# A fused hash attention and SwiGLU kernel on one core: five small moves in its slot plan

## The chip, the cores and the metric

The kernel runs on one core of one Trainium2 chip. The metric is the device time of one execution in microseconds, the median of several runs. A core has a matrix engine (TensorE, "PE" in the profile, with its weight loads as "PEld"), a vector engine (DVE), a scalar engine (ACT), a general engine (POOL) and a queue engine (SP), from which most DMA transfers are issued. Every engine works through its own list of instructions in order, and waits where an instruction needs something that another engine or a transfer has not finished. The matrix engine writes only to PSUM, and DVE or ACT read it from there.

## The reference, cut to what matters

The inputs q, k and v have shape (4, 8, 768, 64): four batches, eight heads, 768 tokens, 64 dimensions per head. A random projection of 6 columns gives each query and key 6 sign bits, and a query attends only to keys with the same bits:

```python
q_bits = (np.einsum('bhsd,dk->bhsk', q, proj) > 0)
mask = q_bucket[:, :, :, None] == k_bucket[:, :, None, :]
scores = np.where(mask, scale * np.matmul(q, k.transpose(0, 1, 3, 2)), -1e9)
attn = softmax(scores)          # with 1e-9 added to the sum
x = np.matmul(attn, v)          # heads side by side: (3072, 512)
xn = x / sqrt(mean(x * x) + 1e-6) * rms_g
out = (silu(xn @ w_gate) * (xn @ w_val)) @ w_out
```

The gate and value weights are 512 x 1536, the output weight is 1536 x 512.

## The kernel before, in words

The work is cut into 8 units. A unit is one half (384 queries) of one batch; units 0 and 1 belong to batch 0, units 2 and 3 to batch 1, and so on. A unit has 8 heads, and each head's 768 keys are handled in three chunks of 256, so a unit has 24 chunks. The program is one long list of **slots**, one chunk each, 192 in all (`NS = 24` to a unit). Slot t issues, on each engine's list, the score products of chunk t+1 (`scores`, line 321: two matmuls into `s_ps`), the exponential of chunk t on ACT (`probs`, line 333), and then whatever the table `plan[t]` holds. The helper `at(0, t, f, ...)` puts a step into that table; steps of one slot run in the order in which they were put there. Nothing reorders this list afterwards; buffers are handed out by the framework, and an instruction waits until its buffer is free.

What the plan holds, by name:

- **Loads.** `load_natural`, `load_v` and `load_blocks` (lines 94, 103, 117) are issued from SP, in order, together with the sends of bits and the stores of results. All q, k and v tiles share 8 buffers (`lpool`). `load_w` (line 520) brings weights in from POOL's queue.
- **Turning.** q and k are needed with the head dimension on the partitions. Batch 0 and the first two pairs of heads of batch 1 are turned on PE (`turn_pe`, line 148, copied out of PSUM by DVE at line 150), the other ten pairs on DVE (`turn_dve`, lines 174 and 181). `cast_part` and `cast_pool` (lines 164, 194) then write them as 16-bit numbers into the tile `QK`, mostly on POOL.
- **Hashes.** The projection runs on PE: `hash_direct` (line 222, tile `d_ps`) for the pairs turned on PE, `hash_one` (line 202) for the ten others. DVE cuts the sign bits out (`signs`, line 211, tile `bits`), and SP sends them by DMA into rows 64 to 69 of `QK` (lines 261 and 281). With the bits appended to the head dimension the score product carries the mask, so the first scores of a pair of heads wait for its bits. `hash_direct` needs the last copy of the turned q, and two of the three PSUM banks of the pool `gps`, which it shares with turned tiles, gates, values and projections.
- **Values.** `v_prep` (line 290) writes v as 16-bit numbers, `v_sum` (lines 296 to 298, POOL) and `v_mean` (line 306, tile `m_ps`, copied to `cvb` at line 309) give a sum over all keys that goes into every output.
- **Attention output.** `av` (line 346, tile `o_ps`) multiplies probabilities and values, in two parts in the slots 3n+4 and 3n+5 for the n-th head of the list. After a pair of heads, `attn_out` (lines 360 to 372) adds `cvb` (`otmp`), takes reciprocals (`rcp`), and writes x and its squares (`sq`), the last two on POOL, but for the last pair of unit 0 on DVE. There is one `o_ps` buffer, so the next pair's `av` waits for `otmp`. `sumsq` (line 376) sums the squares.
- **Norm.** `norm_scale` (lines 388, 392) gives 1/rms, on DVE and then POOL; `norm` (line 401) scales the three thirds of x (128 tokens each) on DVE; `turn_x` (line 408) turns each third on PE, and the result is copied to `xnT` with the gain, by DVE (line 414) or, for one third of units 0 and 7, in four pieces by ACT (line 412).
- **Feed-forward.** `gate` and `value` (line 425, tiles `g_ps`, `v_ps`), with a tanh on ACT (line 433) and two DVE products (lines 442, 443), then `project` (line 454, `y_ps`) and `store` (ACT copy at line 466, DMA at 467).

Unit 0's norm comes earliest: its eight heads run in front (two of them before two heads of unit 1), its x is turned in slot `TX = 37`, and from slot 38 on the feed-forward work of earlier units fills PE beside the attention of later ones. `spread` divides that work over the slots of a unit by weights (330 for scores, 216 per projection matmul, 1000 for a hash and so on); a step in `inserts` (the hashes of ten pairs and the six `v_mean` steps) is put in at the first boundary at or behind its slot. For those ten pairs the table `spots` gives the slot of the load, of the turns of k and of q, and of the hash. `behind_norm` moves a pair's casts, and its `v_prep` and `v_sum`, from the first slots of a unit, where the previous unit's norm is computed, to the unit's slot 7.

The lines that the change touches, and what calls them:

Of the kernel before, what the change touches and what calls it, by code (L numbers as in the profile page):

```python
# [16 lines left out]
H = 8  # L17
# [16 lines left out]
def kernel(  # L34
# [12 lines left out]
    nc = tc.nc  # L47
# [265 lines left out]
    x, xn, xnT = {}, {}, {}  # L313
# [69 lines left out]
    rstds = {}  # L383

    def norm_scale(u):

        ss = spool.tile([128, 3], FP32, name="ss")
        nc.vector.tensor_reduce(
            out=ss, in_=ssp[u % 2].rearrange("p h c -> p c h"), op=ALU.add, axis=AX.X
        )  # L390
        rstd = spool.tile([128, 3], FP32, name="rstd")
        nc.gpsimd.tensor_tensor(out=rstd, in0=ss, in1=mhalf, op=ALU.pow)
        rstds[u] = rstd

    def norm(u):
        if u not in rstds:
            norm_scale(u)
        rstd = rstds.pop(u)
        xn[u] = npool.tile([128, 3, DMODEL], FP16, name="xn")
        for c in range(3):  # L400
            nc.vector.tensor_scalar_mul(xn[u][:, c, :], x[u][:, c, :], rstd[:, c : c + 1])

    def turn_x(u, c, act=False):
        if c == 0:
# [122 lines left out]
    NS = 24  # L527
# [5 lines left out]
    def at(w, s, f, *a):  # L533
        plan[NS * w + s].append(lambda: f(*a))
# [43 lines left out]
    at(0, 0, second_head)  # L578
    at(0, 1, cast_part, 0, 0, "q", 1)
    at(0, 1, v_prep, 0, 0)  # L580
    for hp, s0 in ((1, 2), (2, 8), (3, 14)):
        at(0, s0, new_pair, 0, hp)
        at(0, s0, turn_pe, 0, hp, 0, "k")
        at(0, s0 + 1, turn_pe, 0, hp, 1, "k")
        at(0, s0 + 1, cast_pool, 0, hp, "k")
        at(0, s0 + 2, turn_pe, 0, hp, 0, "q")
        at(0, s0 + 3, turn_pe, 0, hp, 1, "q")
        at(0, s0 + 3, cast_part, 0, hp, "q", 0, 0, 2, nc.vector)
        at(0, s0 + 3, cast_part, 0, hp, "q", 1)
        at(0, s0 + 4, hash_pair, 0, hp)  # L590
        if hp == 1:
            at(0, s0 + 5, send_pair, 0, hp, (1,))
            at(0, s0 + 5, move_head, 0, hp, 0)
        else:
            at(0, s0 + 5, send_pair, 0, hp)
# [1 line left out]
    at(0, 1, load_natural, nc.sync, 0, 3, "q")  # L597
    at(0, 2, load_v, nc.sync, 0, 2)
    at(0, 2, load_v, nc.sync, 0, 3)
    at(0, 8, v_prep, 0, 1, nc.vector)  # L600
    at(0, 13, v_prep, 0, 2, nc.vector)
    at(0, 19, v_prep, 0, 3, nc.vector)
    for hp, t in enumerate((4, 16, 21, 31)):
# [5 lines left out]
        at(0, 39 + 3 * i, load_w, wo, moe_w_out, 6 * i, 6)  # L609


    for hp, ts in ((0, (8, 22, 23, 24, 25, 24, 26, 26, 28, 42)), (1, (17, 27, 28, 29, 30, 29, 41, 32, 33, 43))):
        tl, ts = ts[0], ts[1:]
        for w in "kq":
            at(0, tl, load_natural, nc.sync, 1, hp, w)
        at(0, tl, load_v, nc.sync, 1, hp)
        at(0, ts[0], new_pair, 1, hp)
        for t, hh, w in zip(ts[0:4], (0, 1, 0, 1), "kkqq"):
            at(0, t, turn_pe, 1, hp, hh, w)
        at(0, ts[4], cast_pool, 1, hp, "k")  # L620
        at(0, ts[5], cast_pool, 1, hp, "q")
        if hp == 0:
            at(0, ts[6], hash_pair, 1, hp)
            at(0, ts[7], send_pair, 1, hp)
        at(0, ts[8], v_prep, 1, hp)
        at(0, ts[8], v_sum, 1, hp)

    spots = {
# [11 lines left out]
    TX = 37  # L640
# [7 lines left out]

    at(0, 24, nc.gpsimd.tensor_scalar_mul, gcol, gcol, float(DMODEL) ** 0.5)
    for n, (u, h) in enumerate(order):  # L650
        for part in range(2):
            at(0, 3 * n + 4 + part, av, u, h, part)
        if h % 2:
            if (u, h) == (0, H - 1):

                at(0, 3 * n + 5, o_step, u, h // 2, nc.vector)
                at(0, 3 * n + 5, s_step, u, h // 2)
                at(0, 3 * n + 5, norm_scale, u)
                at(0, 3 * n + 6, hash_only, 1, 1)
                at(0, 3 * n + 6, hash_signs, 1, 1)  # L660
                at(0, 3 * n + 6, norm, u)
                at(0, TX + 1, send_pair, 1, 1)
                at(0, TX - 1, idle, 2, bank)
                at(0, TX, idle, 1, bank)
                for c in range(3):
                    at(0, TX, turn_x, u, c, c == 1)
                continue
            at(0, 3 * n + 5, o_step, u, h // 2)
            at(0, 3 * n + (10 if h < 7 else 7), s_step, u, h // 2)

# [3 lines left out]
    SCORES, AV, PROJ, FEED, TURN, HASH, MEAN = 330, 290, 216, 324, 220, 1000, 120  # L674
    inserts = {spot[3]: (HASH, hash_one, *pair) for pair, spot in spots.items()}
    for b in (1, 2, 3):
        inserts[2 * b * NS + 3] = (MEAN, v_mean, b, 0, 4)
        inserts[2 * b * NS + 18] = (MEAN, v_mean, b, 2, 4)

    def spread(t0, n, pieces):  # L680
        fixed = [SCORES + (AV if (t - 1) % 3 < 2 else 0) for t in range(t0, t0 + n)]
# [23 lines left out]
    for u in range(7):  # L705
        gates = [
            (FEED, f is gate and part == 0, [(0, f, u, ft, part)])
            for ft in range(NF) for f in (gate, value) for part in range(2)
        ]
        if u == 0:  # L710
            t0 = TX + 1
            spread(t0, 2 * NS - t0, gates)
            continue
        t0 = NS * (u + 1)
        at(0, t0 + 4, norm, u)
        pieces = []
        for i in range(9):
            c, n = divmod(i, 3)
            steps = [(0, project, u - 1, c, 4 * n, 4 * n + 4)]
            if n == 2:  # L720
                steps.append((1, store, u - 1, c))
            pieces.append((4 * PROJ, True, steps))
            if i in (6, 7):
                pieces += [
                    (TURN, False, [(0, turn_x, u, c)]) for c in ((0,), (1, 2))[i - 6]
                ]
        spread(t0, NS, pieces + gates)
# [2 lines left out]

    def behind_norm(t):

        return t - t % NS + 7 if 2 <= t % NS < 7 else t

    for (b, hp), (load, kturns, qturns, _) in spots.items():
        at(0, load, load_blocks, nc.sync, b, hp)
        at(0, load, load_v, nc.sync, b, hp)
        at(0, kturns[0], new_pair, b, hp)
        for w, turns in (("k", kturns), ("q", qturns)):
            for i, t in enumerate(turns):  # L740
                at(0, t, turn_dve, b, hp, w, i, len(turns))
            at(0, behind_norm(turns[-1] + 1), cast_pool, b, hp, w)
        t = behind_norm(qturns[-1] + 2)
        at(0, t, v_prep, b, hp)
        at(0, t, v_sum, b, hp)
# [17 lines left out]
    for c in range(2):  # L763
        project(6, c, 0, NF)
        store(6, c)
    norm(7)
    project(6, 2, 0, 4)
    for c, f0, f1 in ((0, 4, 7), (1, 7, 9), (2, 9, NF)):
# [41 lines left out]
```

## Time and profile before

| | |
|---|---|
| median of 3 runs | 339.15 us (339.05 to 339.28) |
| the profiled execution | 339.4 us, of which 337.6 us are the span from first to last instruction |
| busy over the span | PE 98%, DVE 70%, ACT 66%, POOL 44% |
| granted TensorE clock | full in all 40 slices of the span |
| moved by DMA | 30.92 MB, 92 GB/s on the mean |

The profile is one execution, recorded by the hardware. Its page gives busy times by engine, the chain of work that ended last (followed backwards from the last instruction to whatever released it), and groups of instructions by source line. Further views of the same trace are used: the timeline, in which equal neighbours of one engine are merged and a bracket gives the idle time just before and what ended it; the chain in order of time; busy time by stretch; and one tile's or one line's instructions. Times within the trace count from the start of the span. The ends of matmuls are modelled, so matmuls that follow each other overlap in these rows; the chain's rows give the time from one to the next. An instruction that waits for several things is put down to the one that came last.

### The profile page before, as it was taken

How to read it: one execution, taken by the hardware profiler on the slowest of the kernel's cores; microseconds unless marked ns; L12 is line 12 of the kernel's file. 1: busy time of each engine (PE TensorE's matmuls, PEld its weight loads, DVE VectorE, ACT ScalarE, POOL GpSimd, SP SyncE). 2: the span in 40 equal slices, each digit the busy share in tenths (PEclk: the TensorE clock that was granted, in tenths of full speed). 3: DMA queues.
4: the chain of work that ended last, by engine and by line, in shares of the span. 5: the costliest groups of instructions: out<-in, count | busy, mean ns of one | idle time of the engine just before them, and what ended most of it. 6: DMA issues, size and time to landing. Idle time of an engine off the chain costs nothing.

```text
span 337.6 us, 7795 instructions
## 1 busy us (share of the span) xinstructions
PE 329.3 (98%) x3004; PEld 198.3 (59%) x3004; DVE 235.8 (70%) x492; ACT 224.0 (66%) x325; POOL 149.2 (44%) x201
## 2 busy tenths in 40 slices
PE   8898999999999999999999999999999999999996
PEld 4566756655566555655656556565656666664554
DVE  2898696777869558875788658884776446674870
ACT  2788886666677767777667667776667767754322
POOL 3457949427553632746373523738371121112000
PEclk9999999999999999999999999999999999999999
DMA  7944899982818527070816118000200010001002
GB/s 234 328 142 150 129 152 210 229 143 50 185 23 159 109 87 150 12 136 26 148 71 106 42 65 171 7 1 19 83 3 3 2 62 34 0 2 68 28 0 93
DMA packets 79692, 30.92 MB, mean 92 GB/s; under 512 B 64988, under 2 KB 76712, under 8 KB 79656
## 3 DMA queue, kind: packets, MB, share of 16 engines
q1 hardware_dynamic: 75528, 25.45, 31.6%
q0 software_dynamic: 3680, 4.72, 8.4%
q8 instruction: 23, 0.38, 0.5%
q10 hardware_dynamic: 448, 0.27, 0.2%
q14 instruction: 13, 0.11, 0.1%
HBM read 28.32 MB, written 6.29 MB: 103 GB/s over the span
## 4 chain that ended last, share of the span: by engine, by line
PE 91%; DVE 4%; DMA 2%; ACT 1%; issue 1%; SPq 0%; DVEq 0%
PE v_ps L425 18%; PE g_ps L425 18%; PE s_ps L321 17%; PE y_ps L454 17%; PE o_ps L346 10%; PE d_ps L202 3%; PE t_ps L148 2%; PE x_ps L408 2%; PE d_ps L222 2%; DMA qL<-in_q_dram 1%; PE z_ps L515 1%; DVE bits L211 1%; PE y_ps L473 1%; DMA QK<-bits 1%; ACT psb L333 1%
## 5 line engine op out<-in xcount | busy, mean ns | idle before, releaser
L333 ACT ACTIVATE psb<-s_ps,ebias 128x768 f16<-128x768 f32 x192 | 167.5, 899 | 25.0 <-PE s_ps L321 24.3
L321 PE MATMUL s_ps<-QK 70*128 70x384 f16 x384 | 93.9, 326 | 2.5 <-DMA QK<-bits 1.1
L433 ACT ACTIVATE t<-g_ps 128x384 f32<-128x384 f32 x96 | 47.1, 490 | 56.3 <-PE g_ps L425 56.1
L425 PE MATMUL g_ps<-xnT,wg 128*128 128x384 f16 x384 | 82.5, 325 | 0.2
L425 PE MATMUL v_ps<-xnT,wv 128*128 128x384 f16 x384 | 81.7, 325 | 0.3 <-DVE a L442 0.2
L442 DVE SCALAR_TENSOR_TENSOR a<-t,g_ps 128x384 f32<-128x384 f32 x96 | 52.8, 550 | 28.2 <-ACT t L433 26.8
L454 PE MATMUL y_ps<-wo,ht 128*128 128x512 f16 x276 | 68.0, 378 | 0.0
L367 POOL TENSOR_TENSOR x<-otmp,rcp 128x384 f32<-128x384 f32 x31 | 25.7, 829 | 93.1 <-DVE rcp L365 92.9
L346 PEld LDWEIGHTS <-psb 128*128 128x128 f16 x1152 | 52.1, 97 | 16.3 <-issue 1.3
L443 DVE SCALAR_TENSOR_TENSOR ht<-a,v_ps 128x384 f16<-128x384 f32 x96 | 53.2, 554 | 11.7 <-PE v_ps L425 3.2
L346 PE MATMUL o_ps<-vl,psb 128*128 128x65 f16 x1152 | 56.3, 193 | 0.5 <-DVE otmp L360 0.5
L321 PEld LDWEIGHTS <-QK 70*128 70x128 f16 x384 | 34.5, 98 | 36.4 <-issue 11.0
L425 PEld LDWEIGHTS <-wv 128*128 128x128 f16 x384 | 35.2, 97 | 22.6 <-issue 1.8
L425 PEld LDWEIGHTS <-wg 128*128 128x128 f16 x384 | 34.6, 97 | 21.2 <-DVE xnT L414 0.6
L454 PEld LDWEIGHTS <-ht 128*128 128x128 f16 x276 | 24.7, 97 | 22.7
L372 POOL TENSOR_TENSOR sq<-x 128x384 f32<-128x384 f32 x31 | 25.6, 826 | 2.4
L194 POOL CAST QK<-kT 64x768 f16<-64x768 f32 x20 | 16.4, 820 | 22.6 <-DVE kT L174 7.7
L466 ACT COPY ysb<-y_ps 128x512 f32<-128x512 f32 x23 | 13.5, 585 | 18.6 <-PE y_ps L454 18.6
L360 DVE TENSOR_TENSOR otmp<-o_ps,cvb 128x390 f32<-128x390 f32 x32 | 17.9, 559 | 10.0 <-PE o_ps L346 9.7
L194 POOL CAST QK<-qT 64x768 f16<-64x768 f32 x20 | 16.5, 825 | 18.5 <-DVE qT L181 17.1
L376 DVE TENSOR_REDUCE ssp<-sq 128x3 f32<-128x384 f32 x32 | 16.9, 529 | 9.9 <-POOL sq L372 9.9
L414 DVE TENSOR_TENSOR xnT<-x_ps,gcol 128x512 f16<-128x512 f16 x22 | 14.5, 685 | 5.8 <-PE x_ps L408 5.8
(71 smaller groups left out, 262.8 us busy)
## 6 DMA issues: line engine op xcount, KB each, us to landing
vn<-in_v_dram SPq DMA_DIRECT2D x16, 384.0 KB
out_dram<-ysb SPq DMA_DIRECT2D x23, 256.0 KB
qL<-in_q_dram SPq DMA_DIRECT2D x40, 96.0 KB
kL<-in_k_dram SPq DMA_DIRECT2D x40, 96.0 KB
kn<-in_k_dram SPq DMA_DIRECT2D x5, 384.0 KB
qn<-in_q_dram SPq DMA_DIRECT2D x5, 384.0 KB
wg<-in_moe_w_gate_dram POOLq DMA_DIRECT2D x2, 768.0 KB, 7.8
wv<-in_moe_w_val_dram POOLq DMA_DIRECT2D x2, 768.0 KB, 9.6
```

What stands on the lines that cost most here:

```text
L194: nc.gpsimd.tensor_copy(QK[b, 2 * hp + hh, "h"][0:64, o : o + S], src[64 * hh : 64 * hh + 64, :])
L321: nc.tensor.matmul(ps[:, j, 0:HALF], QK[b, h, "h"][0:KROWS, S + jt * 128 : S + (jt + 1) * 128], QK[b, h, "h"][0:KROWS, half * HALF : (half ...
L333: nc.scalar.activation(psb[u, h][:, 2 * ch : 2 * ch + 2, :], sps.pop((u, i))[:, :, 0:HALF], AF.Exp, bias=ebias, scale=ESCALE,)
L346: nc.tensor.matmul(o[:, c, hh, 0:65], psb[u, h][:, jt, c * 128 : (c + 1) * 128], vls[b % 2][:, h, 2 * (jt % 3) + jt // 3 if b in PARITY el ...
L360: nc.vector.tensor_add(tmp[:, :, :, 0:65], o[:, :, :, 0:65], cvb[b % 2][:, 2 * hp : 2 * hp + 2, 0:65].unsqueeze(1).to_broadcast([128, 3, 2 ...
L367: eng.tensor_mul(xd.rearrange("p c (h d) -> p c h d", h=2), tmp[:, :, :, 0:64], r.to_broadcast([128, 3, 2, 64]),)
L372: eng.tensor_mul(sq, xd, xd)
L425: nc.tensor.matmul(ps, w[:, kt, fs], xnT[u][:, kt, :], start=(kt == 0), stop=(kt == 3))
L433: nc.scalar.activation(t, fbank[u, ft, "g_ps"], AF.Tanh, scale=0.5)
L442: nc.vector.scalar_tensor_tensor(out=a, in0=t, scalar=1.0, in1=g, op0=ALU.add, op1=ALU.mult)
L443: nc.vector.scalar_tensor_tensor(out=ht[u][:, ft, :], in0=a, scalar=0.5, in1=vv, op0=ALU.mult, op1=ALU.mult)
L454: nc.tensor.matmul(y, ht[u][:, ft, c * 128 : (c + 1) * 128], wo[:, ft, :], start=(ft == 0), stop=(ft == NF - 1),)
```

## The change

Five moves; no arithmetic is added or taken away.

1. **Unit 0's last sums a slot sooner.** The two `av` parts of unit 0's last head go from slots 31 and 32 to 30 and 31, and with them `o_step`, `s_step`, `norm_scale` (32 to 31), the hash of batch 1's second pair and `norm` (33 to 32). `norm` scales only two thirds of unit 0's x on DVE; the third one is scaled by ACT in slot 37 (`norm_third` with `nc.scalar.mul`), ahead of the turns. Of the three copies to `xnT`, ACT now makes the third instead of the second.
2. **Batch 0's last pair (heads 6 and 7)** is turned, hashed and sent one slot sooner (14 to 13 and on, hash 18 to 17, send 19 to 18), and the `v_prep` of batch 0's second pair, which is on DVE, goes from slot 8 to slot 10.
3. **A load behind bits.** The loads of batch 1's second pair go from slot 17 to slot 20.
4. **Two hashes of batch 1 a slot later.** Pair 2 from 50 to 51, pair 3 from 60 to 61; pair 3's turns go from slots 57, 57, 58, 59 to 55, 56, 57, 58. Since slot 51 held a `v_mean`, the first `v_mean` of batches 1, 2 and 3 goes from a unit's slot 3 to its slot 5.
5. **Casts behind norms.** `behind_norm` now also moves what stands in a unit's slot 1. That is the cast of k of (batch 1, pair 2), from slot 49 to 55, and `v_prep` with `v_sum` of (2, 0), (2, 2) and (3, 2), from slots 73, 97 and 145 to 79, 103 and 151.

```diff
     def norm(u):
         if u not in rstds:
             norm_scale(u)
-        rstd = rstds.pop(u)
         xn[u] = npool.tile([128, 3, DMODEL], FP16, name="xn")
-        for c in range(3):
-            nc.vector.tensor_scalar_mul(xn[u][:, c, :], x[u][:, c, :], rstd[:, c : c + 1])
+        for c in range(3 if u else 2):
+            norm_third(u, c, nc.vector.tensor_scalar_mul)
+
+    def norm_third(u, c, mul):
+        mul(xn[u][:, c, :], x[u][:, c, :], rstds[u][:, c : c + 1])
...
-    for hp, s0 in ((1, 2), (2, 8), (3, 14)):
+    for hp, s0 in ((1, 2), (2, 8), (3, 13)):
...
-    at(0, 8, v_prep, 0, 1, nc.vector)
+    at(0, 10, v_prep, 0, 1, nc.vector)
...
-(1, (17, 27, 28, 29, 30, 29, 41, 32, 33, 43))
+(1, (20, 27, 28, 29, 30, 29, 41, 32, 33, 43))
...
-        (1, 2): (34, (48, 48), (49, 49), 50),
-        (1, 3): (45, (57, 57), (58, 59), 60),
+        (1, 2): (34, (48, 48), (49, 49), 51),
+        (1, 3): (45, (55, 56), (57, 58), 61),
...
+        t = 3 * n + 4 - ((u, h) == (0, H - 1))
         for part in range(2):
-            at(0, 3 * n + 4 + part, av, u, h, part)
+            at(0, t + part, av, u, h, part)
...
-                at(0, 3 * n + 6, hash_only, 1, 1)
-                at(0, 3 * n + 6, hash_signs, 1, 1)
-                at(0, 3 * n + 6, norm, u)
+                at(0, t + 2, hash_only, 1, 1)
+                at(0, t + 2, hash_signs, 1, 1)
+                at(0, t + 2, norm, u)
+                at(0, TX, norm_third, u, 2, nc.scalar.mul)
...
-                    at(0, TX, turn_x, u, c, c == 1)
+                    at(0, TX, turn_x, u, c, c == 2)
...
-        inserts[2 * b * NS + 3] = (MEAN, v_mean, b, 0, 4)
-        inserts[2 * b * NS + 18] = (MEAN, v_mean, b, 2, 4)
+        for s, hp in ((5, 0), (18, 2)):
+            assert 2 * b * NS + s not in inserts
+            inserts[2 * b * NS + s] = (MEAN, v_mean, b, hp, 4)
...
     def behind_norm(t):
-        return t - t % NS + 7 if 2 <= t % NS < 7 else t
+        return t - t % NS + 7 if 1 <= t % NS < 7 else t
```

More of the change, by code (lines that the diff above doesn't have):

```diff
@@ L609 @@
         at(0, 39 + 3 * i, load_w, wo, moe_w_out, 6 * i, 6)
-    for hp, ts in ((0, (8, 22, 23, 24, 25, 24, 26, 26, 28, 42)), (1, (17, 27, 28, 29, 30, 29, 41, 32, 33, 43))):
+    for hp, ts in ((0, (8, 22, 23, 24, 25, 24, 26, 26, 28, 42)), (1, (20, 27, 28, 29, 30, 29, 41, 32, 33, 43))):
         tl, ts = ts[0], ts[1:]
@@ L650 @@
     for n, (u, h) in enumerate(order):
+        t = 3 * n + 4 - ((u, h) == (0, H - 1))
         for part in range(2):
-            at(0, 3 * n + 4 + part, av, u, h, part)
+            at(0, t + part, av, u, h, part)
         if h % 2:
             if (u, h) == (0, H - 1):
-                at(0, 3 * n + 5, o_step, u, h // 2, nc.vector)
-                at(0, 3 * n + 5, s_step, u, h // 2)
-                at(0, 3 * n + 5, norm_scale, u)
-                at(0, 3 * n + 6, hash_only, 1, 1)
-                at(0, 3 * n + 6, hash_signs, 1, 1)
-                at(0, 3 * n + 6, norm, u)
+                at(0, t + 1, o_step, u, h // 2, nc.vector)
+                at(0, t + 1, s_step, u, h // 2)
+                at(0, t + 1, norm_scale, u)
+                at(0, t + 2, hash_only, 1, 1)
+                at(0, t + 2, hash_signs, 1, 1)
+                at(0, t + 2, norm, u)
+                at(0, TX, norm_third, u, 2, nc.scalar.mul)
                 at(0, TX + 1, send_pair, 1, 1)
@@ L665 @@
                 for c in range(3):
-                    at(0, TX, turn_x, u, c, c == 1)
+                    at(0, TX, turn_x, u, c, c == 2)
                 continue
-            at(0, 3 * n + 5, o_step, u, h // 2)
-            at(0, 3 * n + (10 if h < 7 else 7), s_step, u, h // 2)
+            at(0, t + 1, o_step, u, h // 2)
+            at(0, t + (6 if h < 7 else 3), s_step, u, h // 2)
     SCORES, AV, PROJ, FEED, TURN, HASH, MEAN = 330, 290, 216, 324, 220, 1000, 120
```

## The prediction, made before the change was run

> **What bounds the kernel now.** I read the page's busy times first, then busy time by stretch, the chain in order of time, and the timeline where the chain leaves PE.
>
> ```profile
> PE 329.3 (98%) x3004; PEld 198.3 (59%) x3004; DVE 235.8 (70%) x492; ACT 224.0 (66%) x325; POOL 149.2 (44%) x201
> ...
> 20.00:30.00 10.00, 9.45 (x133) 6.38 (x132) 9.26 (x20) 7.97 (x10) 7.44 (x8) 1.00 0.49 155
> ...
> 40.00:50.00 10.00, 9.39 (x129) 6.08 (x128) 8.95 (x20) 8.52 (x14) 5.95 (x8) 1.00 1.02 164
> 50.00:60.00 10.00, 10.00 (x85) 6.34 (x84) 6.55 (x13) 7.16 (x12) 9.09 (x12) 1.00 1.28 207
> ```
>
> The columns of the last three rows are the stretch, its length, then busy time of PE, PEld, DVE, ACT and POOL. From 50 us on PE is full, so there the time is PE's work plus whatever PE waits inside it. Before 50 us PE has gaps, but DVE (9.26 of 10) and ACT (8.52) are nearly full too: a gap of PE closed there counts only if those two can follow.
>
> The "full" stretch hides waits, because modelled ends cover them. The chain's rows (start, time to the next piece) show them in the hashes:
>
> ```profile
> 74.14 1.23 PE d_ps L202 x8
> 90.38 1.86 PE d_ps L202 x8
> 112.38 0.78 PE d_ps L202 x8
> ```
>
> Eight matmuls take 0.78 us at 112.38. The two hashes that the change moves take 1.23 and 1.86, so they hold 0.45 and 1.08 us of waiting on PE. What for, the timeline says:
>
> ```profile
> 72.88 1.60 DVE L174 STREAM_TRANSPOSE qT<-qL 128x384 f32<-128x384 f32 x2
> 74.53 0.14 PEld L202 LDWEIGHTS d_ps<-qT,pj 128*32 128x32 f32 x2 [0.32 <-DVE qT L174]
> ...
> 89.76 1.59 DVE L174 STREAM_TRANSPOSE qT<-qL 128x384 f32<-128x384 f32 x2
> 91.40 0.14 PEld L202 LDWEIGHTS d_ps<-qT,pj 128*32 128x32 f32 x2 [0.57 <-DVE qT L174]
> ```
>
> The last weight load of each hash starts just behind the end of the last DVE turn of q (74.48, 91.35).
>
> **Part 4, the two hashes.** From hash to hash ten slots take 90.38 - 74.14 = 16.24 us, 1.62 a slot. A slot later the hash of pair 2 stands near 75.7, behind other PE work that fills the place, when its q has been turned since 74.48: 0.45 us go. Pair 3's q was ready at 91.35 in slot 60. Its turns now come two, one, one and one slots sooner, and its hash a slot later, so the turns end more than a us ahead: 1.08 us go. Sum -1.53. Given back: pair 3's turns (0.8 us each, half of the 1.59) now come between the copies of xnT and the DVE products of the first gates. What those products lose, a turn at a time, reaches PE only beyond what three PSUM banks buffer. I take a wait of 0.25, nearer to none than to a whole turn, since the turns are no more work than before: **-1.3**; bounds -1.53 (no wait) and -0.3 (a turn and a half, 1.2, all falls on PE).
>
> SP's queue: pair (2, 0)'s nine loads now go out ahead of pair 2's eight bits, which so start up to 6.4 us later (nine issues at the 0.71 of the four sends at 24.59, quoted below). Their first scores are eight slots or 13 us off; nothing. Pair 3's bits go four slots or 6.5 us ahead of their first scores and need about 3; nothing. `v_mean` is one matmul and one DVE copy in another slot; 0, within 0.3 either way.
>
> **Parts 1 to 3, up to 50 us.** These rows carry the sum:
>
> ```profile
> 19.84 0.56 DVE L290 CAST vl<-vn 128x768 f16<-128x768 f32 x1
> 20.93 0.43 PE L346 MATMUL o_ps<-vl,psb 128*128 128x65 f16 x9 [0.49 <-DVE otmp L360]
> 21.45 1.16 DVE L150 COPY qT<-t_ps 128x384 f32<-128x384 f32 x2
> 24.59 2.84 SPq L261 DMA_DIRECT2D QK<-bits  x4
> 27.32 0.48 PE L321 MATMUL s_ps<-QK 70*128 70x384 f16 x2
> 27.82 0.28 DVE L309 TENSOR_SCALAR cvb<-m_ps 128x130 f32<-128x130 f32 x1
> 28.17 0.56 DVE L150 COPY qT<-t_ps 128x384 f32<-128x384 f32 x1
> 28.24 0.49 PE L321 MATMUL s_ps<-QK 70*128 70x384 f16 x2
> 30.09 3.27 ACT L333 ACTIVATE psb<-s_ps,ebias 128x768 f16<-128x768 f32 x4 [0.42 <-PE s_ps L321]
> 30.70 2.91 SPq L261 DMA_DIRECT2D QK<-bits  x4
> 33.98 0.48 PE L321 MATMUL s_ps<-QK 70*128 70x384 f16 x2 [1.06 <-DMA QK<-bits]
> 34.56 3.42 ACT L333 ACTIVATE psb<-s_ps,ebias 128x768 f16<-128x768 f32 x4 [1.21 <-PE s_ps L321]
> ...
> 22.61 0.89 PE d_ps L222 x16
> 28.73 0.94 PE d_ps L222 x16
> ```
>
> *The `v_prep` that goes from slot 8 to 10.* At 19.84 it stands ahead of `otmp`, for which PE waits 0.49 us. That wait goes. But in slot 10 the copy still stands ahead of the second copy of qT, and that one's end (21.45 + 1.16 = 22.61) is where the hash at 22.61 starts. DVE has no idle time in between, so the hash starts no sooner: what slot 10 gains, slot 12 waits. 0; bounds -0.49 and +0.3.
>
> *The last pair a slot sooner.* Its hash too starts with the end of a DVE copy (28.17 + 0.56 = 28.73). Of DVE's list ahead only the `cvb` copy (0.28) falls behind, so the hash may start at 28.45, not a slot sooner, and ends 0.89 on, near 29.3. One set of scores that stood ahead of it (28.24) now stands behind, with an `av` of 0.27 between: 29.6, its exponential at 30.15 (0.55 on, as 33.98 to 34.56). Four exponentials took 3.27, or 0.82 each, so the sixth, slot 24's, can start at 30.15 + 5 x 0.82 = 34.25. Before it was 34.56.
>
> *The load behind bits.* The bits of that pair, issued at 30.70, behind the loads, were waited for until 33.98, or 3.28 us; the pair before went from 24.59 to its use at 27.32, 2.73 us. Sent at 30.4 (28.45, and the 1.97 that lay between 28.73 and 30.70) without the loads ahead they are there near 33.1. The wait of 1.06 goes, but the exponentials are next: at 34.25 they ask for these scores at 33.7. Together these two are worth -0.3; bounds 0 and -1.06. The moved loads are themselves used from slot 27 on, four slots of 0.82 or more behind slot 23's scores at 33.98, near 37.5; k, the first third of what took 28 to 33 (row further down), is there near 36. If that cover of 1.5 us goes, PE waits for what is missing.
>
> ```profile
> 38.61 8.54 ACT L333 ACTIVATE psb<-s_ps,ebias 128x768 f16<-128x768 f32 x10 [0.63 <-PE s_ps L321]
> 42.92 0.48 PE L321 MATMUL s_ps<-QK 70*128 70x384 f16 x2
> 48.49 1.14 ACT L412 ACTIVATE xnT<-x_ps,gcol 128x128 f16<-128x128 f16 x4 [1.33 <-PE x_ps L408]
> 49.67 0.81 PE L425 MATMUL g_ps<-xnT,wg 128*128 128x384 f16 x4
> ...
> L466 ACT COPY ysb<-y_ps 128x512 f32<-128x512 f32 x23 | 13.5, 585 | 18.6 <-PE y_ps L454 18.6
> ```
>
> *The last sums a slot sooner.* From 38.61 ten exponentials run back to back (0.854 each, to 47.15): here ACT sets the pace. The hash of pair (1, 1), 0.89 us, now stands ahead of the scores that began at 42.92, whose exponential was due at 43.73. They come near 43.7 and their exponential near 44.25, less the 0.3 gained: ACT idles some 0.4. DVE's sums hardly move, because `cvb` and the sums of the pair before stand ahead in the same slot. +0.4; bounds 0 and +0.6.
>
> *A third on ACT.* It runs behind exponential 37: 47.15 + 0.59 (the ACT copy of 128x512) = 47.74, turned and waiting for ACT 0.55 later, four pieces in 1.14: 49.4, where ACT ended at 49.63 before. -0.2; bounds -0.5 (the gates take the pieces one by one) and +0.2.
>
> Sum up to 50 us: 0 - 0.3 + 0.4 - 0.2 = **-0.1**; bounds -1.5 and +0.9.
>
> **Part 5, casts behind norms.**
>
> ```profile
> 78.90 2.96 DVE L401 TENSOR_SCALAR xn<-x,rstd 128x512 f16<-128x512 f32 x3 [0.99 <-POOL rstd L392]
> 113.98 0.82 POOL L290 CAST vl<-vn 128x768 f16<-128x768 f32 x1
> 116.78 0.83 POOL L367 TENSOR_TENSOR x<-otmp,rcp 128x384 f32<-128x384 f32 x1
> 120.28 1.28 DVE L401 TENSOR_SCALAR xn<-x,rstd 128x512 f16<-128x512 f32 x3 [0.97 <-POOL rstd L392]
> 122.68 0.45 PE x_ps L408 x8
> ```
>
> Three times `v_prep` and `v_sum` (113.98 to 116.78, 2.8 us) stood ahead of the `x` that the norm waits for; behind the norm they let it start up to 2 us sooner. They then run beside the three scalings. Where POOL casts beside them they take 2.96 us (78.90), else 1.28 (120.28). A gain of 2 and a loss of 1.7 cancel, and PE takes the second and third turn only at 122.68, 1.1 us after the scalings end at 121.56. -0.1 for some smaller waits; bounds -0.4, and 1.7 - 1.1 = +0.6 at each of three norms if the start does not move.
>
> The Trainium skill (SBUF — State Buffer, section "SBUF: two separate sides") calls the port pair shared by DVE and GpSimd an exclusive lock, where the loser fully blocks; the 2.96 beside 1.28 agrees in direction, though whole blocking is not shown. The page speaks against part 5, which puts POOL's casts beside the scalings: the sum would be +1.8 for this part by the lock without a sooner start, -0.1 by the rows.
>
> **Sum.** -1.3 - 0.1 - 0.1 = -1.5. The profiled execution took 339.4 (337.6 of span, 1.8 around); the median is 0.25 lower. 339.4 - 1.5 = 337.9 in that execution, **337.7** against the median of 339.15. A measurement of this kernel tells 0.2% (0.68 us) from no change: the borders are 338.5 and 339.8.
>
> **The rivals.**
>
> *The early moves cost 0.9* (their upper bound): the hash behind a full DVE and the hash between exponentials both cost what they can. Against it: the gap of 1.21 on ACT at 34.56 absorbs most of it. 339.15 - 1.3 + 0.9 - 0.1 = 338.65, same. 0.12.
>
> *The hash's wait moves into the gates*: DVE is late by a turn, and PE waits for banks. Speaking for it: DVE's list there has little air. -0.3 - 0.1 - 0.1: 338.65, same. 0.10.
>
> *Slower scalings at three norms*, as at 78.90, without the sooner start: 339.15 - 1.4 + 3 x 0.6 = 339.55, same. Against it: that the 2.8 us ahead of `x` do go. 0.05. The lock of that page of the Trainium skill would be its reason.
>
> *The early gaps really close*: 0.49 and 1.06 go, ACT and DVE follow. 339.15 - 1.3 - 1.5 = 336.4, faster. 0.10.
>
> *Slower: weights land late.* The moved loads leave SP behind the bits, at about 30.4 + 2.9 = 33.3, and meet the gate and value weights, issued from POOL:
>
> ```profile
> 28.00:33.00 5.00, 4.80 (x73) 3.07 (x70) 4.46 (x11) 4.58 (x6) 4.27 (x5) 1.00 0.75 243
> 33.00:36.00 3.00, 2.02 (x22) 1.75 (x23) 1.03 (x3) 1.79 (x3) 2.73 (x4) 1.00 0.05 8
> 36.00:41.00 5.00, 5.00 (x76) 3.60 (x75) 4.35 (x10) 4.37 (x6) 4.61 (x7) 1.00 1.05 165
> ...
> 37.54 0.80 POOL L520 DMA_DIRECT2D wv<-in_moe_w_val_dram  x1
> ...
> DMA to landing us min/median/max: 8.5/9.6/10.6
> ```
>
> The last two columns of the first three rows are DMA share and GB/s. The loads filled 28 to 33 (0.75 of 5 us), the engines then rested (0.05), and are full from 36 on (1.05). wv lands 8.5 to 10.6 after 37.54, at 46.0 to 48.1, and the first values are due at about 50.3, behind the first gates. If the loads push it back by their whole 1.2 MB (5 us at 243 GB/s) at the 165 GB/s of the later stretch, 7.3 us, wv lands at 53.3 to 55.4 and PE waits 3.0 to 5.1; it decides from 2.2 us of wait on, a push of 4.4 to 6.5. Against it: the pause takes about half of the loads. At 2.5 us of wait 339.15 - 1.5 + 2.5 = 340.2. 0.13.
>
> **Chances and range.** Forecast 0.50, its own range 337.0 to 338.4. Faster 0.50 + 0.10 = 0.60; same 0.12 + 0.10 + 0.05 = 0.27; slower 0.13. The range 336.7 to 339.5 holds the forecast and three cases of "same", and leaves out the late weights and the lower half of the closed gaps, under 0.2.
>
> **What would show it.** Right: both moved hashes take about 0.8 in the chain; no wait for bits near 34; the wait at 20.93 gone, and the next hash not sooner than 22.6; the first gates within 0.5 us of 49.67; an idle ACT of some 0.4 near 44; `rstd` sooner at three norms and their scalings near 3 us. Wrong: waits on `a` or `ht` ahead of gates from 85 to 92, the first gates over 0.5 us off 49.67, or values that wait for wv.

## The result, and the profile after

The median went from 339.27 us (9 runs) to 337.43 us (9 runs, 336.34 to 338.97): ratio 0.9947, 95% interval 0.9927 to 0.9968, 1.8 us less. The forecast was 337.7. The span went from 337.6 to 335.5 us. The profiled execution of after took 338.97 us, 3.5 of it outside the span, against 1.8 of 339.4 before; so the readings below are made inside the span.

First the page's busy times and one of its groups, then busy time by stretch, of the changed kernel (columns as in the prediction):

```profile
PE 327.7 (98%) x3004; PEld 197.9 (59%) x3004; DVE 239.7 (71%) x491; ACT 224.6 (67%) x326; POOL 149.6 (45%) x201
...
L321 PE MATMUL s_ps<-QK 70*128 70x384 f16 x384 | 93.6, 326 | 2.0 <-ACT psb L333 1.5
```

```profile
20.00:30.00 10.00, 9.79 (x128) 6.12 (x127) 9.35 (x21) 7.22 (x10) 7.63 (x9) 1.00 0.38 124
...
40.00:50.00 10.00, 9.42 (x130) 6.05 (x128) 8.51 (x19) 9.05 (x14) 5.69 (x7) 1.00 1.16 185
```

PE's work is the same 3004 matmuls, and between 20 and 30 us PE is busy for 9.79 us where it was busy for 9.45. In this execution no score waits for bits; of the 2.0 us for which PE still idles ahead of scores, 1.5 are put down to ACT's pace, the next limit. The chain in order of time (start, time to the next piece) shows the second moved hash, and where the chain now leaves PE ahead of it:

```profile
77.06 0.88 POOL rstd L392
...
77.97 2.96 DVE xn L403 x3
80.93 0.33 DVE cvb L309
81.26 0.61 DVE xnT L416
...
81.92 0.38 PE x_ps L410 x4
...
91.42 0.78 PE d_ps L202 x8
```

The hash takes 0.78 where it took 1.86. The hash of pair 2, from 74.58 on, is off the chain, as its eight matmuls show in the timeline (first and last): 74.58 to 74.95 + 0.49 = 75.44, with nothing between them to wait for:

```profile
74.58 0.51 PE L202 MATMUL d_ps<-kT,pj 128*32 128x384 f32 x1
...
74.95 0.49 PE L202 MATMUL d_ps<-qT,pj 128*32 128x384 f32 x1
```

But unit 1's norm is now on the chain: DVE's scalings, then the copy to `cvb`, then the copy to `xnT`, for which PE waits at 81.92.

To place the gain I cut each run at three marks that all kernels share: the start of the first score product, of the first gate product, and of the last projection product. In after they stand at 9.39, 48.97 and 332.28. "Early" is the first stretch, "late" the second. The scores of chunk 24, the first ones that need the bits of batch 0's last pair, cut the early stretch in two: "to 24" runs from the first scores to them, "24 on" from them to the first gate product. Each ratio is to executions of before made alongside (medians 339.17 to 339.69), so it is not the quotient of two medians of this table.

```
kernel                  median   ratio to before [95%]     early   to 24   24 on     late
before                  339.27                             40.10   24.41   15.69   284.71
after                   337.43   0.9947 [0.9927, 0.9968]   39.57   24.16   15.41   283.32
e1_hashes_back          338.67   0.9977 [0.9956, 0.9999]   39.83   24.41   15.42   284.76
e2_hashes_alone         338.08   0.9976 [0.9962, 0.9990]   40.48   24.79   15.69   283.51
e3_sums_and_third_back  337.83   0.9965 [0.9949, 0.9981]   40.06   24.37   15.69   283.34
e4_third_back           337.68   0.9957 [0.9941, 0.9974]   39.92   24.17   15.75   283.36
e5_last_pair_back       336.77   0.9895 [0.9858, 0.9932]   39.22   23.81   15.40   283.33
e6_load_back            337.70   0.9929 [0.9904, 0.9955]   39.65   24.25   15.40   283.31
e7_casts_back           337.73   0.9935 [0.9907, 0.9963]   39.71   24.30   15.41   283.50
e8_mean_ahead           336.68   0.9898 [0.9823, 0.9973]   39.55   24.14   15.41   282.99
e9_turns_back           338.55   0.9956 [0.9932, 0.9980]   39.69   24.28   15.41   284.31
e10_best                336.88   0.9915 [0.9894, 0.9936]   39.24   23.83   15.41   283.12
e11_copy_at_10          337.25   0.9932 [0.9905, 0.9959]   39.49   23.86   15.63   283.17
e12_load_alone          338.68   0.9975 [0.9961, 0.9989]   39.52   23.84   15.69   284.78
```

How far these marks repeat can be read from kernels whose programs are the same in a stretch. Late, after, e3, e4, e5 and e6 agree within 0.05 us. From chunk 24 on, the eight kernels after, e1 and e5 to e10 agree within 0.02, and so do before, e2, e3 and e12, which all lack part 1. Up to chunk 24 it is different: after, e1, e3, e4, e7, e8 and e9, all the same there, lie between 24.14 and 24.41, and before and e2 at 24.41 and 24.79. So part 1, whose edits all lie behind chunk 24, can be read to some 0.02 us, but parts 2 and 3, which lie ahead of it, only to 0.3 or 0.4. From before to after: to chunk 24 -0.25 (-0.34 by the means of the equal programs), from there on -0.28, late -1.39.

### The profile page after: what moved, and what is told of

The parts are those of the page before. It is cut to its first block, busy times and chain, and to the rows that moved or that the text cites. A ratio compares the mean times of both kernels' runs of the same rounds, so it can differ in the third digit from the quotient of the medians.

```text
span 335.5 us, 7802 instructions
## 1 busy us (share of the span) xinstructions
PE 327.7 (98%) x3004; PEld 197.9 (59%) x3004; DVE 239.7 (71%) x491; ACT 224.6 (67%) x326; POOL 149.6 (45%) x201
## 4 chain that ended last, share of the span: by engine, by line
PE 84%; DVE 6%; DMA 3%; SPq 2%; POOL 1%; ACT 1%; issue 1%; ACTq 0%; DVEq 0%; POOLq 0%
PE v_ps L427 18%; PE g_ps L427 17%; PE s_ps L321 16%; PE y_ps L456 16%; PE o_ps L346 9%; PE d_ps L202 2%; PE d_ps L222 2%; PE x_ps L410 2%; DMA QK<-bits 1%; SPq L281 1%; DVE xn L403 1%; PE t_ps L148 1%; DMA pj<-in_proj_dram 1%; ACT psb L333 1%; PE y_ps L475 1%
## 5 line engine op out<-in xcount | busy, mean ns | idle before, releaser
L403 DVE TENSOR_SCALAR xn<-x,rstd 128x512 f16<-128x512 f32 x23 | 16.1, 754 | 6.8 <-POOL rstd L392 6.8
```

Source lines behind the costliest of these rows:

```text
L403: mul(xn[u][:, c, :], x[u][:, c, :], rstds[u][:, c : c + 1])
```

## The experiments

e1 to e7 undo or do one part, or half of one, and e8 to e12 follow up what these showed.

**The hashes.** e1 is the changed kernel with the hashes and turns of part 4 back (its `v_mean` stays in slot 5); e2 is the kernel before with part 4 alone.

```diff
-        (1, 2): (34, (48, 48), (49, 49), 51),
-        (1, 3): (45, (55, 56), (57, 58), 61),
+        (1, 2): (34, (48, 48), (49, 49), 50),
+        (1, 3): (45, (57, 57), (58, 59), 60),
```

> The changed kernel with the two hashes and pair 3's turns back in their old slots (50 and 60; 57, 57, 58, 59); all else as changed. Theory (the waits in front of the two hashes are most of the gain): the chain shows them at about 1.2 and 1.8 us again, and the span goes from 335.5 to 336.8 to 337.2. Rival (the gain came from the first 50 us and the hashes only shifted a wait elsewhere): the span stays within 0.5 of 335.5.

> The kernel before with part 4 alone: the two hashes and pair 3's turns in their new slots, the first v_mean of batches 1 to 3 in a unit's slot 5. Theory: both hashes take about 0.8 us, the span goes from 337.6 to 336.1 to 336.5 (1.5 gained, up to 0.4 lost where v_mean's copy now stands behind unit 1's norm). Rival (they only pay together with the early moves): within 0.5 of 337.6.

In e1 the waits are back in the chain:

```profile
73.34 1.19 PE d_ps L202 x8
...
89.54 1.87 PE d_ps L202 x8
```

Late is 284.76 against 283.32: the two hashes are worth 1.44 us, net of what follows. e2 gains 1.20 late by part 4 alone. Over the chunks the gain divides so (from the first score product of one chunk to that of another, before, after, e1, e2): chunks 48 to 52, with pair 2's hash, 7.67, 7.21, 7.63, 7.21; chunks 52 to 57 7.56, 7.98, 7.56, 8.07; chunks 57 to 65, with pair 3's hash, 14.27, 12.89, 14.28, 12.89. Pair 2's 0.46 is won and lost again five chunks on; pair 3 brings 1.38. In e1, whose `v_mean` of batch 1 also stands in the unit's slot 5, nothing is lost between 52 and 57: the loss comes only where PE arrives sooner at unit 1's norm.

**Where pair 2's gain went.** e8 is the changed kernel with the first `v_mean` of batch 1 ahead of the norm, in slot 50.

```diff
-        for s, hp in ((5, 0), (18, 2)):
+        for s, hp in ((5 if b > 1 else 2, 0), (18, 2)):
```

> The changed kernel with the first v_mean of batch 1 in slot 50, ahead of the hash and of unit 1's norm, instead of slot 53. In the changed kernel chunk 52 to chunk 57 takes 7.97 us, in the kernel before 7.57. Theory: v_mean's copy stands behind the three slow scalings on DVE and holds one of three banks, so the third turn of x waits; ahead of the norm it does not: 7.6, and the span falls by 0.3 to 0.5, to 335.0 to 335.3. Rival (the k cast beside the scalings or the later hash is the reason): 7.9 or more, and the span stays.

The timeline of DVE, first of after, then of e8:

```profile
77.97 2.96 DVE L403 TENSOR_SCALAR xn<-x,rstd 128x512 f16<-128x512 f32 x3 [0.99 <-POOL rstd L392]
80.85 0.41 DVE L309 TENSOR_SCALAR cvb<-m_ps 128x260 f32<-128x260 f32 x1
81.19 1.87 DVE L416 TENSOR_TENSOR xnT<-x_ps,gcol 128x512 f16<-128x512 f16 x3
```

```profile
74.03 0.43 DVE L309 TENSOR_SCALAR cvb<-m_ps 128x260 f32<-128x260 f32 x1
...
77.53 2.96 DVE L403 TENSOR_SCALAR xn<-x,rstd 128x512 f16<-128x512 f32 x3 [0.99 <-POOL rstd L392]
80.42 0.67 DVE L416 TENSOR_TENSOR xnT<-x_ps,gcol 128x512 f16<-128x512 f16 x1
```

From the start of the scalings to the first `xnT` it is 3.22 us in after and 2.89 in e8. Chunks 52 to 57 take 7.54 again (48 to 52 0.11 more, the product that moved there), and late falls to 282.99: the copy behind the scalings cost 0.33 us.

**Turns.** e9 is the changed kernel with pair 3's turns back, its hash still in slot 61.

```diff
-        (1, 3): (45, (55, 56), (57, 58), 61),
+        (1, 3): (45, (57, 57), (58, 59), 61),
```

> The changed kernel with pair 3's turns back in slots 57, 57, 58, 59 and its hash left in slot 61. Theory (either half of the move alone takes the wait away, since the turns ended at 91.35 and a slot is 1.62 us): the hash takes about 0.8 us, and chunk 57 to chunk 65 takes 12.9 us as in the changed kernel. Rival (the sooner turns are needed): the hash takes 1.0 or more and the stretch 13.2 to 14.

Rows of e9's timeline:

```profile
88.82 1.58 DVE L174 STREAM_TRANSPOSE qT<-qL 128x384 f32<-128x384 f32 x2
...
90.23 0.55 DVE L444 SCALAR_TENSOR_TENSOR a<-t,g_ps 128x384 f32<-128x384 f32 x1
...
90.84 0.48 PE L427 MATMUL v_ps<-xnT,wv 128*128 128x384 f16 x2 [0.75 <-DVE a L444]
...
92.17 0.51 PE L202 MATMUL d_ps<-kT,pj 128*32 128x384 f32 x1
```

The hash takes 0.78 in e9's chain as well, yet chunks 57 to 65 take 13.90: of 1.38 only 0.37 is won. With two turns in a row DVE reaches the gate product at 90.23, and PE, ahead of the values, waits 0.75 for that product, which frees a bank. I had held that either half of the move would do; that fell. The later hash takes away the wait for q, but with DVE that late PE waits for a bank instead; the turns, one to a slot, are worth 1.0 of it. The other half alone, the sooner turns with the hash in its old slot, was not run.

**Unit 0's sums and the third on ACT.** e4 is the changed kernel with all three thirds on DVE, and ACT again copying the second third of `xnT`; e3 also puts the last sums back, so it lacks the whole of part 1. (The lines with `t` are e3's alone.)

```diff
-        for c in range(3 if u else 2):
+        for c in range(3):
...
-        t = 3 * n + 4 - ((u, h) == (0, H - 1))
+        t = 3 * n + 4
...
-                at(0, TX, norm_third, u, 2, nc.scalar.mul)
...
-                    at(0, TX, turn_x, u, c, c == 2)
+                    at(0, TX, turn_x, u, c, c == 1)
```

> The changed kernel without part 1: unit 0's last sums, its norm and the hash of pair (1, 1) a slot later as before, and all three thirds on DVE. From the first scores to the first gates it is 40.10 us in the kernel before and 39.58 in the changed one. Theory of the prediction (the sums cost 0.4, the third gives 0.2): 39.4, that is 0.2 sooner without part 1. Rival (part 1 gave most of the early gain): 39.8 to 40.1.

> The changed kernel with only the third put back: all three thirds of unit 0's x scaled on DVE and the second copy on ACT, the sums still a slot sooner. First scores to first gates is 39.58 in the changed kernel. Theory of the prediction (the third gives 0.2): 39.8. Rival (the third is worth more, because it takes a scaling off the end of DVE's list where DVE sets the end): 40.0 to 40.3.

From chunk 24 on it is 15.69 without part 1, 15.75 with the sums alone and 15.40 to 15.42 with both: the sums cost 0.06, the third gives 0.34, and part 1 as a whole gives 0.28, about half of the early gain. By the whole early stretch the sums would seem to gain 0.14 (40.06 in e3, 39.92 in e4), but the scores of chunk 24, up to which these two programs are the same, are 0.20 later in e3 (24.37, 24.17): that difference is scatter. The rows of after:

```profile
43.87 3.27 ACT L333 ACTIVATE psb<-s_ps,ebias 128x768 f16<-128x768 f32 x4 [0.28 <-PE s_ps L321]
47.02 0.74 ACT L403 ACTIVATE xn<-x,rstd 128x512 f16<-128x512 f32 x1
48.29 1.14 ACT L414 ACTIVATE xnT<-x_ps,gcol 128x128 f16<-128x128 f16 x4 [0.53 <-PE x_ps L410]
...
46.54 1.04 DVE L403 TENSOR_SCALAR xn<-x,rstd 128x512 f16<-128x512 f32 x2
...
48.97 0.84 PE L427 MATMUL g_ps<-xnT,wg 128*128 128x384 f16 x4
49.64 0.65 PE L427 MATMUL v_ps<-xnT,wv 128*128 128x384 f16 x3
```

ACT idles 0.28 ahead of exponential 34, where 0.4 was foretold, and exponential 37 ends 13.59 us behind chunk 24's scores instead of 13.18. That hardly reaches the gates, because x is turned when DVE has scaled it, and DVE's scalings start in e3 and in e4 at

```profile
46.73 1.43 DVE L403 TENSOR_SCALAR xn<-x,rstd 128x512 f16<-128x512 f32 x3
```

```profile
46.54 1.43 DVE L403 TENSOR_SCALAR xn<-x,rstd 128x512 f16<-128x512 f32 x3
```

which, from the scores of chunk 24 (33.81 and 33.56), is 12.92 and 12.98. So the sums come no sooner. Rows of e4, its chain and then ACT's timeline, show why, and that ACT has time to spare there:

```profile
42.03 0.29 DVE cvb L309
...
42.70 0.56 DVE otmp L360
...
46.54 1.05 DVE xn L403 x2
```

```profile
48.13 1.14 ACT L414 ACTIVATE xnT<-x_ps,gcol 128x128 f16<-128x128 f16 x4 [0.98 <-PE x_ps L410]
```

DVE's copy to `cvb` stands ahead of the last pair's `otmp`, and from there DVE's list is nearly full up to the scalings. ACT still idles 0.98 ahead of its pieces of `xnT` (1.33 in before), waiting for PE's turned x. With the third on ACT, DVE starts its copies to `xnT` one scaling sooner. ACT's last four pieces end at 49.43 in after, while the gates start at 48.97: PE takes the pieces one by one.

**The last pair, the copy and the load.** e5 is the changed kernel without part 2; e6 has the load back at slot 17; e12 is the kernel before with part 3 alone.

```diff
-    for hp, s0 in ((1, 2), (2, 8), (3, 13)):
+    for hp, s0 in ((1, 2), (2, 8), (3, 14)):
...
-    at(0, 10, v_prep, 0, 1, nc.vector)
+    at(0, 8, v_prep, 0, 1, nc.vector)
```

> The changed kernel without part 2: batch 0's last pair turned and hashed a slot later as before (14 and on), the DVE copy of v back in slot 8. First scores to first gates is 39.57 in the changed kernel and 39.83 in the run with the hashes back, which is the same program up to there; to the scores of chunk 24 it is 24.16 and 24.41. Theory of the prediction (the pair's move is given back by the exponentials, only the loads behind the bits pay): chunk 24 at 23.9 to 24.4, the gates at 39.4 to 39.8, no loss. Rival (the pair has to be sooner for its bits to land in time): chunk 24 at 24.6 or more, the gates at 40.0 or more.

> The changed kernel without part 3: the loads of batch 1's second pair back in slot 17, ahead of the bits. Theory of the prediction (bits behind these loads take 3.28 us instead of 2.73): sent at the same time as in the changed kernel they land at the time at which the exponentials ask for them, so at most 0.3 is lost: chunk 24 at 24.2 to 24.6, gates 39.6 to 40.1. Rival (the loads alone made the wait): chunk 24 at 24.9 or more.

> The kernel before with part 3 alone: the loads of batch 1's second pair in slot 20 instead of 17, behind the bits. Theory of the runs so far (this move takes away the whole wait for the bits where the pair is left in its old slot): chunk 24 at 23.8 from the first scores instead of 24.41, gates at 39.5 instead of 40.10, span near 337.0. Theory of the prediction (the exponentials ask next, 0.3 for this and the sooner pair together): chunk 24 at 24.1 or later.

e12, the load alone: chunk 24 at 23.84 from the first scores, 0.6 sooner than in before (0.8 by the mean of before and e2). e6, part 2 without the load: 24.25, within the range of after's equal programs. e5, the load without part 2: 23.81, 0.35 sooner than in after (0.45 by the mean of the equal programs). So either move takes most of the wait away, the load does more by itself than both together, and with the load moved part 2 only costs. Rows of after (PE's chain, then DVE's timeline):

```profile
21.97 1.29 PE d_ps L222 x16
...
27.91 1.24 PE d_ps L222 x16
```

```profile
21.27 0.58 DVE L290 CAST vl<-vn 128x768 f16<-128x768 f32 x1
21.78 0.54 DVE L150 COPY qT<-t_ps 128x384 f32<-128x384 f32 x1
...
24.18 0.55 DVE L150 COPY kT<-t_ps 128x384 f32<-128x384 f32 x1
24.65 1.06 DVE L290 CAST vl<-vn 128x768 f16<-128x768 f32 x1
...
26.09 0.54 DVE L150 COPY kT<-t_ps 128x384 f32<-128x384 f32 x1
```

and those of e5 (PE's chain, then DVE's timeline):

```profile
22.01 0.89 PE d_ps L222 x16
...
28.13 0.89 PE d_ps L222 x16
```

```profile
25.16 0.54 DVE L150 COPY kT<-t_ps 128x384 f32<-128x384 f32 x1
...
26.31 0.52 DVE L150 COPY kT<-t_ps 128x384 f32<-128x384 f32 x1
```

In after each of the two hashes holds a wait of 0.35 to 0.40 for DVE; in e5 both run through. In the first the copy of v stands between the two copies of q. That only gives back what slot 8 had gained: chunk 14 starts 13.75 from the first scores, in e5 13.86. In the second the pair's turns now share slot 13 with another copy of v, so the second copy of k starts 1.91 us behind the first (1.15 in e5).

What the sooner pair costs shows at chunk 19. Its scores now stand behind the pair's hash, at 19.97 from the first scores instead of 18.67 in e5. In both kernels a run of exponentials starts at 20.5 from the first scores, in after with chunk 19's, in e5 with chunk 20's. So ACT comes to chunk 24's later, at 24.75 instead of 24.40.

Neither after nor e5 shows a wait for these bits. In after the load leaves SP behind the bits, and the scores that waited until 33.98 before start with no wait:

```profile
30.27 2.78 SPq L261 DMA_DIRECT2D QK<-bits  x4
33.10 0.45 SPq L94 DMA_DIRECT2D kn<-in_k_dram  x1
...
33.56 0.48 PE L321 MATMUL s_ps<-QK 70*128 70x384 f16 x2
```

But it is close: e1, the same program up to there, has for these scores

```profile
33.43 0.48 PE L321 MATMUL s_ps<-QK 70*128 70x384 f16 x2 [0.28 <-DMA QK<-bits]
```

and e7 and e9 wait for bits there for 0.18 and 0.16.

**Casts behind norms.** e7 is the changed kernel without part 5.

```diff
-        return t - t % NS + 7 if 1 <= t % NS < 7 else t
+        return t - t % NS + 7 if 2 <= t % NS < 7 else t
```

> The changed kernel without part 5: the k cast of (1, 2) and v_prep with v_sum of (2, 0), (2, 2), (3, 2) ahead of the norms again. Theory of the prediction (a start 2 us sooner and scalings 1.7 us longer cancel, PE has air): rstd of unit 2 comes 1.8 us later, its scalings take 1.3 instead of near 3, the whole differs by less than 0.2 from first to last scores. Rival (the lock between DVE and POOL costs PE at the norms): 0.3 or more is gained by undoing it. Where the k cast is the reason for what unit 1's norm lost (chunk 52 to chunk 57 takes 7.97 instead of 7.57), that goes back to 7.6.

Late is 283.50 against 283.32: part 5 is worth 0.18, of which 0.09 falls to chunks 65 to 96, with unit 2's norm (50.15 against 50.06), and 0.07 to chunks 52 to 57. Unit 2's norm in e7, then in after:

```profile
117.20 0.86 POOL L392 TENSOR_TENSOR rstd<-ss,mhalf 128x3 f32<-128x3 f32 x1 [0.88 <-DVE ss L388]
118.10 1.28 DVE L403 TENSOR_SCALAR xn<-x,rstd 128x512 f16<-128x512 f32 x3 [0.97 <-POOL rstd L392]
```

```profile
115.50 0.86 POOL L392 TENSOR_TENSOR rstd<-ss,mhalf 128x3 f32<-128x3 f32 x1 [0.88 <-DVE ss L388]
116.32 0.82 POOL L290 CAST vl<-vn 128x768 f16<-128x768 f32 x1
...
116.39 2.76 DVE L403 TENSOR_SCALAR xn<-x,rstd 128x512 f16<-128x512 f32 x3 [0.97 <-POOL rstd L392]
```

Counted from each kernel's first gate (48.82 and 48.97), the norm's `rstd` starts 1.85 us sooner, the scalings last 1.48 longer, and their end comes 0.38 sooner. Chunks 52 to 57 take 8.05 in e7, so the cast of k beside unit 1's norm is not why after loses there.

**Towards a better kernel.** e10 is the changed kernel without part 2 and with the `v_mean` of e8; e11 is e10 with the copy of v in slot 10 again.

> The changed kernel without part 2 and with the first v_mean of batch 1 in slot 50: the two edits that gained 0.34 and 0.36 from first to last scores by themselves. Theory (they are in different stretches and add): from first scores to the start of the last projection 322.2, against 322.89 in the changed kernel and 324.82 in the one before; span near 334.3; time 0.987 to 0.992 of the kernel before. Rival (what is gained before 50 us is waited for again at unit 1's norm): 322.5 or more.

> The best kernel with one half of part 2 put back in: the DVE copy of v in slot 10, the last pair left a slot later. Theory of the prediction (what slot 10 gains, slot 12 waits: 0): chunk 12 at 11.2, chunk 14 at 13.75 to 13.9, chunk 24 at 23.8, gates at 39.2, as without it. Rival (it keeps PE ahead, so it gains): gates at 39.0 or less; or it costs beside a POOL cast: gates at 39.4 or more.

e10's early and late together are 322.36 us, against 322.89 of after, 322.55 of e5 and 322.54 of e8: of 0.34 and 0.35 some 0.53 of 0.69 adds up. The rest is lost between chunks 57 and 65 (13.04 against 12.89 in e8), at one place, the weight load for the first scores that need pair 2's bits:

```profile
86.77 0.13 PEld L321 LDWEIGHTS <-QK 70*128 70x128 f16 x2 [0.35 <-issue]
```

SP sends the first of these bits at 83.69, 3.1 us before (in e8 4.8 before, without such idle time), behind the loads of pair (2, 0). That these bits are waited for is the likely cause; the row does not name it. In the medians e5, e8 and e10 (336.77, 336.68, 336.88) all lie below after (337.43), but can't be told from each other.

e11 has chunk 24 at 23.86, as e10 (23.83): up to there the copy in slot 10 costs nothing, as the prediction had it, and what part 2 costs by chunk 24 is the pair's. The 0.25 of e11's early stretch come behind chunk 24 (15.63 against 15.41), at unit 0's norm. There DVE's product for x meets a cast on POOL and takes longer, in e11 and then in e10:

```profile
42.96 0.74 DVE L367 TENSOR_TENSOR x<-otmp,rcp 128x384 f32<-128x384 f32 x1
```

```profile
43.37 0.56 DVE L367 TENSOR_TENSOR x<-otmp,rcp 128x384 f32<-128x384 f32 x1
```

DVE's scalings start 0.22 later for it. The rival that the copy costs beside a POOL cast is what e11 shows, though not in the slot that it was meant for, and not in after, where it is 15.41.

## Why the prediction was right, and which of its steps were not

The sum came out at -1.8 against -1.5, and its largest term for the reason given: the two hashes no longer wait for q. But four terms missed. Behind 50 us two misses cancel, so that the agreement there (-1.39 for -1.4) is partly luck; ahead of 50 us two add up, and more came than was forecast. One sign that the prediction had named for being wrong came true: the first gates start at 48.97, 0.70 from 49.67 (0.53 counted from the first scores), and they come sooner.

- **Hashes, -1.3: mechanism right, size too low.** The waits of 0.45 and 1.08 went as worked out. The 0.25 given back in the gates did not come: chunks 57 to 65 gained 1.38, 0.3 more than the hash's wait. With the 0.46 of pair 2 that is 1.84; the 1.44 of e1 is what unit 1's norm left of it. e9 shows that the turns, one to a slot, also spare waits elsewhere; beyond the one of 0.75 it isn't located which.
- **`v_mean`, "0, within 0.3 either way": wrong.** It cost 0.33 (e8), since its DVE copy stands between the scalings of unit 1's norm and `xnT`. The prediction priced the instructions and not what is queued behind them, and it did not ask what PE, freed of pair 2's wait, would meet next. e1 has the copy in the same place and loses nothing, so it is the two together. Batch 2's later `v_mean` probably costs 0.1 more: chunks 104 to 120 take 26.43 in e2, which changes nothing else there, and 26.32 in before.
- **Pair 2's bits behind nine loads, nothing: right, but with less to spare than was said.** In after their first scores do not wait. But the first bits leave SP at 83.16 instead of 75.99, 7.2 us later for the "up to 6.4", and 4.0 before those scores; with 3.1 left, in e10, the weight load idles.
- **The `v_prep` moved to slot 10, 0: right.** The wait for `otmp` went (chunk 12 starts 0.47 sooner), and the hash two slots on took it back (chunk 14 starts only 0.12 sooner). This hash did start sooner than the 22.6 that was asked for, at 21.97, but took 1.29 instead of 0.89.
- **Last pair sooner and load behind bits, -0.3 together: right in the sum (-0.25 to -0.34), wrong in who earns it.** The load alone is worth -0.6 to -0.8 (e12); with it, part 2 adds +0.35 to +0.45 (e5). The path was as drawn: scores behind the hash, no long wait for bits, then ACT's exponentials set the pace. But the prediction did not price the load without the pair, where one exponential fewer stands behind the hash, and it did not see the copy of v that already stood in slot 13.
- **Last sums sooner, +0.4: the path was wrong.** ACT's idle time came (0.28 for 0.4), and DVE's sums hardly moved, as foretold. But the prediction carried ACT's delay on to the gates, and DVE's norm, not ACT, decides when x can be turned: its own row at 48.49 has ACT idle for 1.33 ahead of `xnT`. Measured +0.06 (e4).
- **A third on ACT, -0.2: right in sign, low in size**, measured -0.34. The scaling on ACT took 0.74, not the 0.59 of the ACT copy that I took for it; the gates, which take ACT's pieces one by one, made up for it.
- **Casts behind norms, -0.1: right**, measured -0.18; the sooner start (1.85, "up to 2") and the longer scalings (1.48 for 1.7) nearly cancel.

So up to 50 us the sum was -0.1 and the measured one -0.5 to -0.6, and from there on it was -1.4 and the measured one -1.39. Two slips of the sums changed nothing: the bounds -1.5 and +0.9 of the early part are not those of its four terms, which add up to -2.05 and +1.1, and the rival of the slower scalings, at 339.55, lies just outside the range that was said to hold it.

The rivals: the early moves' full cost and the gates' new waits did not appear. The closing gaps came in part: the wait for bits went, but ACT's pace kept most of its 1.06, and the wait for `otmp` closed and was given back. The weights did not land late: the first values at 49.64 follow the gates without a wait. The slower scalings came at nearly their full size (2.76), yet with the sooner start, so no time was lost. The scalings of unit 2 took 0.67, 1.03 and 1.22 us each beside POOL's instructions and 0.48 each in e7. The Trainium skill (SBUF — State Buffer, section "SBUF: two separate sides") has the shared port pair taken for a whole instruction while the other side fully blocks. Scalings that grow by up to 0.74, less than one POOL cast (0.82), agree with it, though no row names who waited. The sum hardly changes, since the POOL work that now collides stood ahead of the norm before.

## What to carry to other kernels

When a wait on the busiest engine is removed, follow that engine to its next meeting with another chain: here the 0.46 us won at a hash was lost five chunks later at a norm, until one 0.41 us copy was moved out of that norm. Price a moved step by what is queued behind it on its own engine, above all a copy that comes to stand between two parts of something that is needed whole. When two moves aim at the same wait, run each alone: either may do the work, and the second may then only cost. When a price is smaller than the scatter of a mark, look for a nearer mark behind which it falls: here the stretch from chunk 24 on repeats within 0.02 us, and it turns the sign of one price.

## What the runs showed of the hardware that was not expected

- The same program took 24.14 to 24.41 us from the first scores to those of chunk 24 in seven kernels, and between there and the first gates 15.40 to 15.42 in eight; the 283 us behind repeated within 0.05 in five kernels. In three of the seven (e1, e7, e9) the scores of chunk 24 wait 0.16 to 0.28 for bits, so part of the scatter is when a DMA of bits lands.
- An ACT scaling of 128x512 from 32-bit to 16-bit numbers with a factor for each partition took 0.74 us, where an ACT copy of 128x512 out of PSUM took 0.585.
- A hash of 16 matmuls took 0.89 us when its operands were all there and 1.24 to 1.29 when the last copy came late. A late operand shows as a longer hash and as idle time of the weight loads (0.31 at 22.37 in after), not of PE.
